# Moving feature transfers to two queues, and tile splits and gates to the first phase, in a gated mix of linear attention and a squared-relu MLP

## The chip, the cores and the metric

The kernel runs on one core of a Trainium2 chip. The metric is the device time of one execution in microseconds (us), lower is better; the time before is the median of three runs. All times below are in us unless another unit is given. TensorE (PE in the profile) multiplies matrices, VectorE (DVE) and GpSimd (POOL) do elementwise work, ScalarE (ACT) evaluates functions and copies, and SyncE (SP) only issues DMA transfers. DMA transfers can also be issued from ScalarE's and GpSimd's queues.

## What is computed

The sequence has 2048 rows of 512 numbers. With sigmoid, softmax over 16 numbers, and relu squared, the reference is, cut to what matters:

```python
g = sigmoid((x * gate_w).sum(-1, keepdims=True))
q, k, v = heads(x @ wqkv)                       # 32 heads of 16
pq, pk = q @ w_phi, k @ w_phi                   # per head, 16 x 16
phi_q = concat(softmax(pq), softmax(-pq))       # 32 features per head
phi_k = concat(softmax(pk), softmax(-pk))
kv = einsum("sf,sd->fd", phi_k, v); z = phi_k.sum(rows)
a = ((phi_q @ kv) / (phi_q @ z + 1e-6)) @ wo
h = relu(x @ w1 + b1) ** 2                      # 2048 x 1792
out = g * a + (1 - g) * (h @ w2 + b2)
```

## The kernel before

A product of two fp32 matrices is made of three matmuls (`mm3`): each operand is split into a high part (rounded to fp32r, ScalarE) and a low part (the rest, a subtraction on VectorE or GpSimd), and high x high, high x low and low x high are summed. `split` (line 391) does this for one 128 x 512 tile: one ScalarE copy and one subtraction.

The rows are four blocks of 512 (b = 0 to 3), the 1792 hidden columns 14 tiles of 128 (f = 0 to 13). The work has two phases.

The first phase makes two streams of products, both with a Strassen-like scheme of seven products over 2 x 2 blocks. The u stream (`u_step`, line 537) makes `h`: r = 0 gives blocks 0 and 1, then r = 1 blocks 2 and 3, and each step g of it gives two f (2g and 2g + 1) for two blocks, four tiles. `hidden` (line 531) finishes a tile: ScalarE takes relu with bias into a buffer named `row` (there are five), squares it in place, and SyncE stores it to DRAM (`hkept`). The v stream (`v_step`) makes the key features and values, and `kv_burst` sums their products in PSUM. Split w1 tiles are kept in DRAM (`wkept`) by r = 0 and loaded back by r = 1.

The second phase takes the blocks in the order 2, 3, 0, 1 (`ORDER_B`), and within a block the tiles in the order f = 2, 3, ..., 13, 0, 1 (`turned`). For each tile, `h_ready` (line 778) loads it from `hkept` into a buffer of a ring of four, and splits it into the operand buffers O0h, O0l, O1h, O1l (each twice, so that four tiles are held). `down` multiplies it with `w2`, four products of 128 rows each. Between these tiles lie the steps of the attention, by pairs p of 128-row chunks (two pairs in a block):

- `kv_done` (line 694): the summed keys and values go through DRAM (`zrow`) to be broadcast over the partitions (`vext`), and into the matrix `kvb`. Its four DMA transfers are on ScalarE's queue.
- `do_q` (line 801): the query product of a chunk and its exponentials `e` with their sums.
- `transposed` (line 811): `q_phi` multiplies `e` with `vext` on GpSimd (`ez`), VectorE sums it to the denominators (`dz`, `den`), scales `e` and transposes it in blocks of 32 into `tb`. After the second chunk of a pair, sixteen quarter-size pieces are carried from `tb` to `phiT`: four by a ScalarE copy (same partitions) and twelve by a DMA of 64 KB on SyncE's queue.
- `do_n` (line 829): 32 small matmuls of `kvb` with `phiT`, then a split; `attend` (line 853) multiplies the result with `wo` and adds it to the output row.
- `gates` (line 711), once for each block: four loads of `xn` (one buffer), for each a multiply with `gwb` and sum on VectorE, then sigmoid's exponential and a few small steps. `q_phi` of that block needs its results `inv` and `eps`.
- `wo_ready` (line 752): `wo` in four tiles, each made of four transfers of 64 KB (32 rows each), then split.

The program order is not the order of the engines. All operations are first added to a `Plan` (line 131), which walks a simulated clock with assumed lengths (`lengths`, line 191; `landing`, line 215, for transfers). Each operation gets a due time, counted back from the place of TensorE's products in program order; at each step of the clock, an engine takes the operation due soonest among those ready, and TensorE takes the earliest ready of the next five products (`LOOK`). An operation may have a choice of queues: `either` is VectorE or GpSimd. Loads from DRAM are held back until 45 before their due time (`HORIZON`), except those of `xn` (`op.early`); `gwb` is held back too. At most eight transfers are in flight in the plan. Each engine then runs its operations in the order so found, and waits in that order.

In the profile nearly all instructions have line 350, where the plan issues them, so tiles are told apart by name.

Of the kernel before, what the change touches and what calls it, by code (L numbers as in the profile page):

```python
# [17 lines left out]
P = 128  # L18
S, D, H, DH, F = 2048, 512, 32, 16, 1792
NK = D // P  # L20
SB = 512
# [11 lines left out]
LOOK = 5  # L33
HORIZON = 45.0


# [69 lines left out]
def region(ap):  # L106

    view = isinstance(ap, View)
    if not view and ap.space == DRAM:
        lo, hi = ap.offset, ap.offset + sum((c - 1) * s for s, c in ap.ap)  # L110
        return ap.tensor.name, lo, hi, 1
    width = ap.base.n if view else 1
    for n in () if view else ap.tensor.shape[1:]:
        width *= n
    p0, at = divmod(ap.offset, width)
    step, n = ap.ap[0]
    bits = 1
    for s, c in reversed(list(ap.ap)[1:]):
        if s:
            bits = sum(bits << k * s for k in range(c)) if s >= bits.bit_length() else any_of(bits, s, c)  # L120
    return ap.base.tag if view else ap.tensor.name, p0, p0 + (n - 1) * max(step // width, 1 if n > 1 else 0), bits << at

# [8 lines left out]
class Plan:  # L131
# [7 lines left out]
    def __init__(self, nc):  # L139
        self.nc, self.ops, self.seen, self.group = nc, [], {}, 0  # L140
        self.held, self.before = {}, {}
        self.tensor, self.vector, self.scalar = Queue(self, "tensor"), Queue(self, "vector"), Queue(self, "scalar")
        self.gpsimd, self.sync, self.either = Queue(self, "gpsimd"), Queue(self, "sync"), Queue(self, "vector", "gpsimd")
        self.const_aps = nc.const_aps

# [3 lines left out]
    def add(self, names, method, args, kw):  # L149
# [7 lines left out]
        op.size = max(free_size(a) for a in aps)  # L157
        op.early = method == "dma_start" and reads[0].space == DRAM and reads[0].tensor.name != "in_xn"
        wide = [a for a in reads if free_size(a) > 1]
# [31 lines left out]
    def lengths(self, op, engine):  # L191
        n = op.size
        if op.method == "dma_start":
            issue = {"sync": 0.45, "scalar": 0.36, "gpsimd": 0.7}[engine]
            return issue, issue
# [31 lines left out]
    def order(self):  # L227
# [74 lines left out]
        while len(done) < len(ops):  # L302
            best = None
            for e in ("vector", "scalar", "gpsimd", "sync"):
                for op in waiting[e]:
                    if op.start is not None:
                        continue
                    t = max(free[e], op.ready, op.due - HORIZON if op.early else 0.0)
                    if op.two:
                        t = max(t, lock)  # L310
                    if op.method == "dma_start" and len(flight) >= 8:
                        t = max(t, flight[-8])
                    if best is None or t < best[0] - 1e-9:
                        best = (t, e)
# [12 lines left out]
            for op in waiting[e]:  # L327
                s = max(free[e], op.ready, op.due - HORIZON if op.early else 0.0)
                if op.two:
# [33 lines left out]
def tile_gated_mix(ctx: ExitStack, tc: tile.TileContext, xT, xn, wqT, wkT, wphi, wv, wo, w1, b1, w2, b2, gw, out):  # L363
# [57 lines left out]
    wkept4 = dram.tile([NPF, 2, P, 256], F32, name="wkept4")  # L421
    hkept = dram.tile([NB, NF, P, SB], F32, name="hkept")
    vext = [const(f"vext{i}", H * VW + 32 - VW) for i in range(2)]
# [107 lines left out]
    def hidden(b, f, src, t=None):  # L531
        t = row() if t is None else t
        nc.scalar.activation(t, src, AF.Relu, bias=b1c[:, f:f + 1])
        nc.scalar.activation(t, t, AF.Square)
        nc.sync.dma_start(hkept[b, f], t)

# [215 lines left out]
    def wo_ready():  # L752
        tags = ("XS40h", "XS40l", "XS41h", "XS41l", "wo2", "O2l", "Vt5", "O2h")
        for k in range(NK):
            t = row()
            for q in range(4):
                s = 64 * (4 * (k % 2) + q) + 32 * (k // 2)
                nc.sync.dma_start(t[32 * q:32 * q + 32, :], wo[s:s + 32, :])
            hl = [operand(tag) for tag in tags[2 * k:2 * k + 2]]
# [51 lines left out]
    def transposed(p, c):  # L811
# [8 lines left out]
        for j in range(4):  # L820
            for r in range(4):
# [4 lines left out]
                else:  # L826
                    nc.sync.dma_start(dst, src)

# [268 lines left out]
```

## Time and profile before

| | |
|---|---|
| Median of three runs | 501.35 (500.74 to 501.95) |
| The profiled execution, its own time | 501.8 |
| Its span, first to last instruction | 500.0 |
| TensorE busy | 487.1 (97%) |
| VectorE busy | 396.6 (79%) |
| ScalarE busy | 254.6 (51%) |
| GpSimd busy | 153.1 (31%) |
| Moved by DMA | 91.87 MB, mean 184 GB/s |
| Mean granted TensorE clock | 0.993 |

A line of the timeline gives the start, the length, the engine, the operation and its tiles (written <- read). An engine's name with a q (SPq, ACTq) is its queue issuing a DMA. A row of the waits reads: who waited, for whom, total, times, longest. A row of a group gives the count, the total busy time and the mean in ns of one, then the idle time before it. A DMA group gives the size of one and the median time from issue to landing. The chain of waits is followed back from the last instruction, and shows in order of time what each step waited for.

### The profile page before, as it was taken

Reading aid. Unit: us, or ns where it says so; the run is one execution under the profiler, and the core shown is the slowest. Engines: PE = TensorE matmul, PEld = TensorE weight load, DVE = VectorE, ACT = ScalarE, POOL = GpSimd, SP = SyncE. Lnnn points to the kernel's source line nnn. Section 1 sums busy time; section 2 is a strip of 40 time slices with the busy share of each in tenths; the row PEclk is TensorE's granted clock in tenths of the full one; section 3 lists DMA queues with packets and bytes.
Section 4 is the critical chain, followed back from the end, with each engine's and each line's share of the span. In section 5 each row is a group of like instructions: output and inputs, shape, how many; then the busy total and the mean of one; then the engine's idle time right before and its main releaser. Section 6 shows DMA issues by size and latency. Waiting matters only on the chain.

```text
span 500.0 us, 9484 instructions
## 1 busy us (share of the span) xinstructions
PE 487.1 (97%) x3538; PEld 390.9 (78%) x3538; DVE 396.6 (79%) x572; ACT 254.6 (51%) x447; POOL 153.1 (31%) x129
## 2 busy tenths in 40 slices
PE   9999999999999999999999499998999999999997
PEld 4878888888888888888888277877878787878786
DVE  4997999778665746689989988899999988897323
ACT  5897966478554465689432344152444333344210
POOL 1022145048300000166277355243452524231000
PEclk9999999999999999999999899999999999999999
DMA  8999997434554783687644374436536330345302
GB/s 273 386 398 352 361 347 262 148 126 152 189 149 155 266 264 117 219 286 212 203 139 125 94 265 148 127 100 173 170 119 206 120 91 16 84 148 174 102 1 84
DMA packets 56518, 91.87 MB, mean 184 GB/s; under 512 B 7192, under 2 KB 16664, under 8 KB 56472
## 3 DMA queue, kind: packets, MB, share of 16 engines
q1 hardware_dynamic: 55536, 89.81, 54.8%
q10 hardware_dynamic: 904, 1.45, 0.9%
q8 instruction: 28, 0.46, 0.4%
q14 instruction: 18, 0.15, 0.1%
q0 software_dynamic: 32, 0.01, 0.0%
HBM read 51.91 MB, written 33.03 MB: 170 GB/s over the span
## 4 chain that ended last, share of the span: by engine, by line
PE 80%; DVE 7%; DMA 7%; ACT 2%; SPq 2%; issue 1%; POOL 0%; ACTq 0%; DVEq 0%; POOLq 0%
PE uB L350 21%; PE uA L350 12%; PE uE L350 12%; PE vB L350 11%; PE vA L350 9%; PE vE L350 9%; PE kv L350 6%; DMA row<-in_wo 2%; SPq L350 2%; DMA KT11l<-in_xT 1%; DVE e L350 1%; DMA wkept<-O0l 1%; DMA vext<-zrow 1%; DMA tb<-in_xT 1%; ACT row L350 1%
## 5 line engine op out<-in xcount | busy, mean ns | idle before, releaser
L350 POOL TENSOR_TENSOR ez<-e,vext 128x512 f32<-128x512 f32 x32 | 42.9, 1361 | 38.3 <-ACT e L350 28.7
L350 POOL TENSOR_TENSOR O1l<-ring,O1h 128x512 fp32r<-128x512 f32 x15 | 19.8, 1319 | 93.3 <-ACT O1h L350 92.5
L350 ACT ACTIVATE e<-e 128x512 f32<-128x512 f32 x54 | 31.4, 622 | 28.9 <-DVE e L350 28.9
L350 DVE TENSOR_REDUCE sm<-e 128x64 f32<-128x1024 f32 x27 | 32.8, 1215 | 10.5 <-ACT e L350 10.4
L350 ACT ACTIVATE O1h<-ring 128x512 fp32r<-128x512 f32 x33 | 20.7, 627 | 39.3 <-PE uB L350 13.4
L350 ACT ACTIVATE O0h<-ring 128x512 fp32r<-128x512 f32 x33 | 20.6, 626 | 31.2 <-PE uB L350 17.3
L350 ACT ACTIVATE row<-row 128x512 f32<-128x512 f32 x56 | 34.2, 626 | 0.6
L350 ACT ACTIVATE phiT<-tb 32x512 f32<-32x512 f32 x32 | 20.1, 629 | 23.9 <-DVE tb L350 23.6
L350 POOL TENSOR_TENSOR O0l<-ring,O0h 128x512 fp32r<-128x512 f32 x14 | 19.3, 1379 | 35.4 <-ACT O0h L350 35.4
L350 DVE TENSOR_TENSOR O1l<-ring,O1h 128x512 fp32r<-128x512 f32 x18 | 16.6, 919 | 11.6 <-ACT O1h L350 11.6
L350 DVE TENSOR_REDUCE ends<-vB 128x32 f32<-128x512 f32 x28 | 18.0, 680 | 8.7 <-PE vB L350 8.7
L350 DVE TENSOR_TENSOR O0l<-ring,O0h 128x512 fp32r<-128x512 f32 x19 | 15.4, 808 | 10.0 <-ACT O0h L350 10.0
L350 DVE TENSOR_REDUCE dz<-ez 128x64 f32<-128x1024 f32 x16 | 19.3, 1208 | 3.5 <-POOL ez L350 3.5
L350 DVE TENSOR_TENSOR e<-e,w 128x1024 f32<-128x1024 f32 x16 | 21.6, 1349 | 0.3
L350 DVE TENSOR_REDUCE ends<-vA 128x32 f32<-128x512 f32 x20 | 12.8, 681 | 10.2 <-PE vA L350 10.0
L350 DVE STREAM_TRANSPOSE tb<-e 128x1024 f32<-128x1024 f32 x16 | 19.7, 1232 | 0.0
L350 DVE RECIPROCAL r<-sm 128x64 f32<-128x64 f32 x32 | 17.4, 544 | 0.6
L350 DVE TENSOR_TENSOR e<-vB,ends 128x1024 f32<-128x1024 f32 x12 | 14.4, 1203 | 0.2
L350 DVE TENSOR_TENSOR e<-e,r 128x1024 f32<-128x1024 f32 x11 | 14.5, 1323 | 0.1
L350 DVE SCALAR_TENSOR_TENSOR xn<-xn,gwb 128x512 f32<-128x512 f32 x16 | 11.8, 736 | 1.2 <-DMA xn<-in_xn 1.2
L350 ACT ACTIVATE row<-uB,b1c 128x512 f32<-128x512 f32 x13 | 8.8, 680 | 6.9 <-PE uB L350 6.9
L350 ACT ACTIVATE row<-uA,b1c 128x512 f32<-128x512 f32 x13 | 8.9, 681 | 6.2 <-PE uA L350 6.1
(1132 smaller groups left out, 1650.7 us busy)
## 6 DMA issues: line engine op xcount, KB each, us to landing
hkept<-row SPq DMA_DIRECT2D x56, 256.0 KB, 3.9
ring<-hkept SPq DMA_DIRECT2D x56, 256.0 KB, 2.8
phiT<-tb SPq DMA_DIRECT2D x96, 64.0 KB, 2.0
xn<-in_xn SPq DMA_DIRECT2D x16, 256.0 KB, 3.2
out<-row SPq DMA_DIRECT2D x15, 256.0 KB, 3.5
ring<-in_w SPq DMA_DIRECT2D x11, 256.0 KB, 4.5
tb<-in_xT SPq DMA_DIRECT2D x8, 256.0 KB, 5.9
wkept<-O0h SPq DMA_DIRECT2D x6, 256.0 KB, 4.8
```

Of the source, the lines that this page charges most:

```text
L350: call(*map(real, op.args), **{k: real(a) for k, a in op.kw.items()})
```

## The change

- The twelve `phiT` transfers of a pair may be issued on SyncE's or ScalarE's queue (`nc.queues`); the plan chooses.
- `wo` comes in four transfers of 256 KB, each reading four blocks of 32 rows through a rearranged view, instead of sixteen of 64 KB.
- Loads of `xn` and `gwb` may start 160 before they are due. So far `xn` had no limit, and `gwb` 45, and the gates need both.
- 32 of the 56 tiles of `h` (blocks 2 and 3: f from 2 to 11; blocks 0 and 1: f from 8) are split in the first phase: after the square, a ScalarE copy into one of two slots (`b2b` and `wo2`, by turns of f // 2), a subtraction in place on VectorE or GpSimd, and two stores for one. The second phase loads both parts straight into the operand buffers.
- The plan's assumed length of a DMA issue on SyncE and ScalarE becomes 0.6 where the source's runs are shorter than 512 numbers, else 0.42 (so far 0.45 on SyncE and 0.36 on ScalarE).
- `region`, which tells the plan what an access touches, now counts further steps over partitions.

```diff
+PARTED = 8
...
     bits, more = 1, 0
     for s, c in reversed(list(ap.ap)[1:]):
-        if s:
+        if s >= width:
+            more += (c - 1) * (s // width)
+        elif s:
...
+        self.queues = Queue(self, "sync", "scalar")
...
-        op.early = method == "dma_start" and reads[0].space == DRAM and reads[0].tensor.name != "in_xn"
+        op.ahead = float("inf")
+        if method == "dma_start" and reads[0].space == DRAM:
+            op.ahead = 160.0 if reads[0].tensor.name in ("in_xn", "in_gw") else HORIZON
...
-            issue = {"sync": 0.45, "scalar": 0.36, "gpsimd": 0.7}[engine]
+            issue = 0.7 if engine == "gpsimd" else 0.6 if run_of(op.args[1]) < D else 0.42
...
-                    t = max(free[e], op.ready, op.due - HORIZON if op.early else 0.0)
+                    t = max(free[e], op.ready, op.due - op.ahead)
...
-    hkept = dram.tile([NB, NF, P, SB], F32, name="hkept")
+    hkept = dram.tile([NB, NF, 2, P, SB], F32, name="hkept")
...
         nc.scalar.activation(t, t, AF.Square)
-        nc.sync.dma_start(hkept[b, f], t)
+        if not parted(b, f):
+            nc.sync.dma_start(hkept[b, f, 0], t)
+            return
+        hi = slot(("b2b", "wo2")[f // 2 % 2], F32R)
+        split(t, hi, t.bitcast(F32R), nc.either)
+        nc.sync.dma_start(hkept[b, f, 0], ff(hi))
+        nc.sync.dma_start(hkept[b, f, 1], t)
+
+    def parted(b, f):
+
+        return 2 <= f < 12 if b >= 2 else f >= PARTED
...
             t = row()
-            for q in range(4):
-                s = 64 * (4 * (k % 2) + q) + 32 * (k // 2)
-                nc.sync.dma_start(t[32 * q:32 * q + 32, :], wo[s:s + 32, :])
+            blocks = wo.rearrange("(t q r i) n -> t r q i n", t=2, q=4, r=2)
+            load(t, blocks[k % 2, k // 2])
...
-        split(load(ring(), hkept[b, f]), hi, lo, nc.either)
+        if not parted(b, f):
+            split(load(ring(), hkept[b, f, 0]), hi, lo, nc.either)
+            return
+        for j, o in enumerate((hi, lo)):
+            nc.sync.dma_start(ff(o), hkept[b, f, j])
...
-                    nc.sync.dma_start(dst, src)
+                    nc.queues.dma_start(dst, src)
```

More of the change, by code (lines that the diff above doesn't have):

```diff
@@ L116, in region @@
     step, n = ap.ap[0]
-    bits = 1
+    bits, more = 1, 0
     for s, c in reversed(list(ap.ap)[1:]):
-        if s:
+        if s >= width:
+            more += (c - 1) * (s // width)
+        elif s:
             bits = sum(bits << k * s for k in range(c)) if s >= bits.bit_length() else any_of(bits, s, c)
-    return ap.base.tag if view else ap.tensor.name, p0, p0 + (n - 1) * max(step // width, 1 if n > 1 else 0), bits << at
+    return ap.base.tag if view else ap.tensor.name, p0, p0 + more + (n - 1) * max(step // width, 1 if n > 1 else 0), bits << at
 def any_of(bits, s, c):
@@ L327, in order @@
             for op in waiting[e]:
-                s = max(free[e], op.ready, op.due - HORIZON if op.early else 0.0)
+                s = max(free[e], op.ready, op.due - op.ahead)
                 if op.two:
```

## The prediction

> **What bounds the kernel now.** I read the page first, then busy time by stretch, TensorE's waits, the chain of waits, and the timeline where the chain leaves TensorE.
>
> ```profile
> span 500.0 us, 9484 instructions
> PE 487.1 (97%) x3538; PEld 390.9 (78%) x3538; DVE 396.6 (79%) x572; ACT 254.6 (51%) x447; POOL 153.1 (31%) x129
> ```
>
> TensorE idles for only 12.9 us of the span, so nothing that relieves another engine counts unless it removes some of these. The next view says where they lie: per stretch its length, then busy time of PE, PEld, DVE, ACT and POOL, the granted clock, the DMA share and GB/s.
>
> ```profile
> 0.00:37.50 37.50, 36.03 (x139) 25.67 (x140) 28.95 (x51) 29.84 (x54) 5.77 (x17) 1.00 0.97 352
> 37.50:65.00 27.50, 27.50 (x242) 22.53 (x241) 23.33 (x39) 24.50 (x46) 7.50 (x6) 1.00 0.98 361
> 65.00:140.00 75.00, 75.00 (x819) 61.72 (x818) 61.97 (x77) 45.52 (x82) 31.59 (x27) 1.00 0.56 191
> 140.00:225.00 85.00, 85.00 (x741) 70.04 (x740) 55.45 (x77) 51.33 (x89) 9.66 (x7) 1.00 0.65 214
> 225.00:278.65 53.65, 53.65 (x479) 43.83 (x477) 49.31 (x68) 26.61 (x48) 28.84 (x22) 1.00 0.51 159
> 278.65:290.20 11.55, 4.71 (x39) 2.57 (x39) 10.48 (x14) 4.63 (x9) 5.11 (x4) 0.70 0.57 165
> 336.50:340.00 3.50, 2.14 (x35) 0.86 (x35) 3.50 (x6) 0.63 (x1) 2.46 (x2) 1.00 0.69 167
> 487.50:500.00 12.50, 9.29 (x47) 7.73 (x45) 4.68 (x7) 0.00 (x0) 0.00 (x0) 1.00 0.22 84
> ```
>
> The idle time is 1.47 at the start, 6.84 in one hole after 278.65, 1.36 near 338 and 3.21 at the end. Start and end are not touched by the change. The two holes in between are what can be won, and the waits of TensorE name their cause:
>
> ```profile
> PE vB L350 <- DMA phiT<-tb: 3.8, 1, 3.8
> PE vE L350 <- DMA phiT<-tb: 3.1, 1, 3.1
> PE vE L350 <- DVE den L350: 1.4, 1, 1.4
> ```
>
> Both are `do_n`, which multiplies the rearranged query features `phiT` with `kvb`. The timeline of TensorE prices the large hole in full:
>
> ```profile
> 278.42 0.39 PE L350 MATMUL kv<-XS31h,XA221l 128*128 128x512 f32 x1
> ...
> 290.20 0.39 PE L350 MATMUL uE<-KB221h,O1l 128*128 128x512 f32 x1
> 290.43 0.40 PE L350 MATMUL uB<-KB221h,O1h 128*128 128x512 f32 x1
> ```
>
> Matmuls of 512 columns start 0.23 apart, so TensorE was free at 278.65 and was back in step at 290.20, 11.55 later. In between lie a `do_n` and five matmuls. A `do_n` with its data there takes about 1.0 (next fence, first start of its main part to the next product), five matmuls 1.15. So 9.4 is lost: 6.84 as idle time, the rest because the granted clock was 0.70 over the stretch and work ran slowly after the waits.
>
> ```profile
> 338.85 0.37 PE L350 MATMUL vE<-phiT,kvb 64*32 64x256 f32 x1 [1.36 <-DVE den L350]
> ...
> 339.87 0.50 PE L350 MATMUL uA<-KB211h,O1h 128*128 128x512 f32 x1
> ```
>
> What `do_n` waited for is in the chain of waits, and in the timeline of SyncE:
>
> ```profile
> 242.57 5.74 DMA vext<-zrow
> ...
> 251.51 2.30 POOL ez L350 x2
> ...
> 284.11 2.04 DMA phiT<-tb
> ```
>
> ```profile
> 276.93 7.77 SPq L350 DMA_DIRECT2D phiT<-tb  x12
> ```
>
> The summed keys and values (`vext`) land at 248.31; GpSimd starts the denominators at 251.51; SyncE has the transposed features at 276.93 and issues twelve transfers one after another, 0.65 each; the last is issued at 284.11 and lands at 286.15. That is 7.5 after TensorE was free.
>
> **The change part by part.** The twelve `phiT` transfers may go on SyncE's or ScalarE's queue. ScalarE also makes four copies of the same rearrangement, 0.63 each (the row of the first below), 2.5 in all.
>
> ```profile
> 276.94 0.63 ACT L350 ACTIVATE phiT<-tb 32x512 f32<-32x512 f32 x1 [5.80 <-DVE tb L350]
> ```
>
> If ScalarE makes its copies and issues four transfers (2.5 + 4 x 0.65 = 5.1) while SyncE issues eight (5.2), the queue ends 2.6 sooner. The bounds are 0 (the planner leaves all on SyncE) and 3.9 (six and six, the copies hidden); I take 2.6. What ScalarE does behind an issue is evictions and exponentials; it was busy 26.61 of 53.65 before the hole, so there is room.
>
> The Trainium skill speaks against this part: DMA: Bandwidth & Descriptors, section Issuing engines are not separate DMA queues, says that all issuers share the same 16 DMA engines and that a second issuer saves only issue time, which is usually small beside the transfer. Here the rows say otherwise, 7.77 of issue against 2.04 of flight. By the rule the 2.6 would be close to 0.
>
> Twenty of the 32 tiles that are split early are those of blocks 2 and 3 with f from 2 to 11, and the second phase starts with block 2 at f = 2. So its first ten tiles need no split. The gates leave this place as well. Two rows from the stretch between `vext` and the transposition, in which VectorE has hardly a gap:
>
> ```profile
> 256.68 1.44 DVE L350 TENSOR_TENSOR O1l<-ring,O1h 128x512 fp32r<-128x512 f32 x1
> ...
> 259.29 0.68 DVE L350 SCALAR_TENSOR_TENSOR xn<-xn,gwb 128x512 f32<-128x512 f32 x1
> ```
>
> These two are 2.1 on the chain and both go. The bounds are 0 (the list fills the place with something due sooner) and 4 (a second split and GpSimd's splits go too; the 1.44 is dearer than the mean below, so the two engines slow each other here). I take 2.1 and 0.5 for the last point.
>
> `wo` comes in four transfers of 256 KB for sixteen of 64 KB. Between `vext` landing and the first denominator lie 3.2, in which GpSimd stood behind the split of a `wo` tile. I take 1.8 of it, since another GpSimd job of 1.4 (the mean of one further below) may stand there; bounds 3.2 and -2 (if the `wo` tiles come later, ScalarE's copy of them holds what is queued behind it: `zrow`, `vext` and the exponentials).
>
> Sum for the hole: 2.6 + 2.1 + 0.5 + 1.8 = 7.0 of 7.5. So `do_n` is 0.5 late and waits too little to lose the clock (the 1.36 near 338 left it at 1.00). Gain 9.4 - 0.5 = 8.9.
>
> The 1.36 near 338 is named for VectorE, but there too twelve transfers stood on SyncE:
>
> ```profile
> 329.38 7.62 SPq L350 DMA_DIRECT2D phiT<-tb  x12
> ```
>
> They end at 337.00, and with 2.04 of flight at 339.0, which is when `do_n` went on (338.85). With 2.6 less this wait goes: 1.4.
>
> The new work in the first phase: 32 copies on ScalarE, 32 subtractions on VectorE or GpSimd, 32 more stores, 8.4 MB.
>
> ```profile
> L350 ACT ACTIVATE O0h<-ring 128x512 fp32r<-128x512 f32 x33 | 20.6, 626 | 31.2 <-PE uB L350 17.3
> ...
> L350 POOL TENSOR_TENSOR O0l<-ring,O0h 128x512 fp32r<-128x512 f32 x14 | 19.3, 1379 | 35.4 <-ACT O0h L350 35.4
> L350 DVE TENSOR_TENSOR O1l<-ring,O1h 128x512 fp32r<-128x512 f32 x18 | 16.6, 919 | 11.6 <-ACT O1h L350 11.6
> ```
>
> That is 32 x 0.63 = 20 on ScalarE and 29 (all on VectorE) to 44 (all on GpSimd). The twenty tiles of blocks 2 and 3 fall mostly into 140 to 225, where ScalarE was busy 51 of 85 and GpSimd 10 of 85; the twelve of blocks 0 and 1 (from f = 8) mostly into 65 to 140, where ScalarE was busy 46 of 75 and GpSimd 32 of 75. The 16 gate steps (16 x 0.68 = 11) find room on VectorE there too; their 16 loads go out on SyncE between the stores, and the one of `gwb` on ScalarE, a few tenths each, with a queue that is mostly empty in front of them. The cover is thin only before 65, where the DMA engines were at 0.98. I charge 0.7, half of what TensorE idled in the busiest part (1.47 before 37.5); bounds 0 and 3. In the second phase 32 tiles take two loads for one load and a split: one more issue of some 0.4 on SyncE, behind which stand `phiT` and the stores of the output, while SyncE loses half of its `phiT` issues.
>
> All together: 501.8 (the profiled execution: span 500.0 and 1.8 around it) - 8.9 - 1.4 + 0.7 = 492.2. The median of the three runs is 0.45 below the profiled one, which gives **491.8**. The floor, with both holes gone and half the idle of the start, is 501.8 - 9.4 - 1.4 - 0.7 - 0.45 = 489.8.
>
> **The rivals.** First, `do_n` stays late. Without a gain from the second queue (chance 0.06) 2.6 and the 1.4 come back, 495.8, and some 1.5 (of the 9.4 - 6.84 = 2.6) more if the wait grows past 3 and the clock drops as it did after the waits of 3.8 and 3.1: 497.3. The rows of issue and flight speak against it. Or `wo` is late (chance 0.13):
>
> ```profile
> hkept<-row SPq DMA_DIRECT2D x56, 256.0 KB, 3.9
> ```
>
> An ordinary 256 KB transfer is issued once and lands in 3.9. But the new source of `wo` is a view of four blocks of 32 rows. If it moves on four of the 16 DMA engines, each carrying 65.5 KB at 23 GB/s (361 GB/s at a share of 0.98, by 16), one transfer takes 2.85 and four in line 11.4, twice the 5.74 of `vext`, with ScalarE's copies, and what is queued behind them, waiting for it. The term of 1.8 goes, or turns into -2, and behind a wait of over 3 the clock drops as well: 493.6 to 497.5.
>
> The Trainium skill, DMA: Bandwidth & Descriptors, section Why a DMA increments its semaphore by 16 and not by 1, states such a rule: the engines used are the largest number up to 16 that divides the outermost size of both sides, which is 4 here. No transfer of before shows it at this size.
>
> Second, the other side: the early splits stall the first phase. The high halves use two slots, and the four tiles of one step of f share one. Two of them are stored 1.2 apart:
>
> ```profile
> 148.29 0.38 SPq L350 DMA_DIRECT2D hkept<-row  x1
> 148.76 0.38 SPq L350 DMA_DIRECT2D O1l<-wkept  x1
> 149.49 0.32 SPq L350 DMA_DIRECT2D hkept<-row  x1
> ```
>
> The slot is held for 0.63 of copy, 0.38 of issue and 3.9 to landing, 4.9 together, so the second tile's copy must stand 3.7 back. If ScalarE waits there in order, evictions wait behind it: two such waits, 7.4, in each of 8 groups. It decides once TensorE feels 1.3 of a group's 7.4 (10.3 of gain by 8); if it feels a quarter, 1.85, it is 15 in all and the time 491.8 + 15 = 506.8. For it: ScalarE's order is fixed beforehand and 3.9 is a median. Against it: the planner knows of the store and puts the copy behind it, ScalarE has 34 free of 85 there, and TensorE did not wait once after 37.5 in this phase.
>
> Third, nothing much: the new order of the list opens other holes at later `do_n` or at the change of phase, as large as those it closes, 498 to 501.5.
>
> **How the numbers follow.** Forecast (490 to 493.5) 0.65; `do_n` late (493.5 to 498) 0.19; nothing much 0.08; slower 0.08. The range to 497 takes in the forecast and most of the first rival. About 0.2%, 1 us, is what a measurement can tell, since the three runs lie 1.2 apart. Half of the third case is faster by that: faster 0.87, same 0.04, slower 0.09.
>
> **What would show it.** Right: no wait of TensorE on `phiT` above 1 us, the twelve transfers of a pair over in about 5 on two queues, PE clock 1.00 after 280, first ten loads of the second phase without a copy behind them, TensorE's idle time 3 to 5. Wrong: a wait of over 2 at the first `do_n`; ScalarE standing for `wo` for several us around 240; waits of TensorE between 60 and 225 after ScalarE's copies, above all in groups of f.

## The result and the profile after

The changed kernel takes 508.11 (median of four runs, 507.64 to 509.88) where the kernel before took 501.65 beside it (four runs, 500.74 to 502.37). The ratio is 1.0124, 95% interval 1.0090 to 1.0158: about 6.2 us slower, where 491.8 was forecast. The profiled execution took 508.11.

The page of the changed kernel, first lines:

```profile
span 506.3 us, 9599 instructions
PE 490.6 (97%) x3538; PEld 391.6 (77%) x3538; DVE 384.2 (76%) x567; ACT 250.5 (49%) x447; POOL 159.7 (32%) x134
```

TensorE idles for 15.7 (12.9 before), and its busy time grew by 3.5 although it runs the same 3538 matmuls. Part of that is the granted clock: it was 0.50 for 10.2 in all (3.4 each from 233.1, 287.7 and 455.0), where before it was 0.50 for 6.8 (from 283.1); this makes 1.7 of the 3.5, and where the rest comes from is not shown. Busy time by stretch shows the places (the columns are those of the prediction):

```profile
140.00:225.00 85.00, 84.21 (x733) 68.36 (x734) 60.75 (x93) 57.62 (x102) 22.14 (x17) 1.00 0.83 277
225.00:240.00 15.00, 12.53 (x246) 9.67 (x248) 11.59 (x19) 9.97 (x20) 8.66 (x8) 0.89 0.76 257
262.00:278.00 16.00, 14.28 (x62) 11.26 (x61) 14.75 (x24) 1.78 (x3) 7.36 (x6) 1.00 0.56 170
278.00:291.00 13.00, 10.71 (x66) 7.58 (x65) 7.45 (x10) 7.09 (x13) 3.88 (x4) 0.87 0.77 238
448.00:460.00 12.00, 10.06 (x64) 7.13 (x63) 10.96 (x16) 5.05 (x9) 5.49 (x4) 0.86 0.68 202
```

The one large hole at the first `do_n` has become smaller, and four places that were full before have holes: the end of the first phase (225 to 240), 268, 308 and 451. To put a number on each, I took TensorE's timeline and summed, from the start of each row to the start of the next, what goes beyond 0.227 for a 512-column product, 0.12 for 256 columns and 0.04 for smaller ones. This lost time holds the waits and the slow clock; where small products stand close together a row is good to some tenths:

| Stretch | Before | After |
|---|---|---|
| 0 to 62 | 5.5 | 5.2 |
| 62 to 225 | 1.4 | 3.0 |
| 225 to 262 | 0.8 | 4.4 |
| 262 to 275 | 0.0 | 2.2 |
| 275 to 295 (first `do_n`) | 9.9 | 5.2 |
| 295 to 330 | 0.9 | 2.6 |
| 330 to 345 | 2.7 | 0.9 |
| 345 to 440 | 2.7 | 2.6 |
| 440 to 462 | 0.9 | 4.8 |
| 462 to the end | 0.9 | 0.9 |
| sum | 25.7 | 31.8 |

The difference, 6.1, accounts for the 6.3 by which the span grew. The smaller loss at the first `do_n` is no gain, though. Its features are complete at 286.89, later than before (286.15), and TensorE only comes to it later, after the losses ahead of it:

```profile
283.74 0.39 PE L356 MATMUL uB<-KB220h,O0l 128*128 128x512 f32 x1
...
287.03 0.37 PE L356 MATMUL vE<-phiT,kvb 64*32 64x256 f32 x1 [1.25 <-DMA O0h<-hkept]
```

TensorE was free for it at 283.97, 5.3 later than before (278.65). Up to 295 the changed kernel has lost 20.0, the kernel before 17.6. The waits of TensorE name different causes, none of them of the size of before:

```profile
PE vB L356 <- DVE e L356: 2.5, 1, 2.5
PE uA L356 <- ACT O1h L356: 1.9, 1, 1.9
PE uA L356 <- DMA O1h<-hkept: 1.7, 1, 1.7
PE uA L356 <- ACT ring L356: 1.4, 1, 1.4
PE vE L356 <- DMA O0h<-hkept: 1.3, 1, 1.3
PE vB L356 <- ACT phiT L356: 1.0, 1, 1.0
```

The row that names the load O0h is that of 287.03, and the name is wrong: `do_n` reads only `phiT` and `kvb`. The last of this pair's `phiT` transfers was issued by ScalarE at 283.18, and the trace's record of semaphores has it landed at 286.89. So two of these waits, 1.3 and 1.0, are for `phiT`.

Four of the places were followed to their beginnings. First the middle, 240 to 290, in the chain of waits of the changed kernel:

```profile
241.00 10.11 DMA row<-in_wo
...
251.12 9.03 DMA row<-in_wo
...
261.36 1.35 DVE KT41l L356
...
263.85 0.62 DVE xn L356 x2
...
264.91 5.08 DMA O1h<-hkept
```

Two transfers of `wo`, 10.11 and 9.03 for 256 KB each, lead straight to the wait at 268: the copy of the last `wo` tile, behind it on ScalarE the copy KT41h, its subtraction on VectorE, an `e` and a gate step there, the next `xn` load on SyncE that waits for the gate step's buffer, and behind that the load O1h for which TensorE waits. ScalarE's own timeline shows what stood behind `wo` there:

```profile
247.91 0.63 ACT L356 ACTIVATE XS41h<-row 128x512 fp32r<-128x512 f32 x1 [4.13 <-DMA row<-in_wo]
247.92 0.53 ACTq L356 DMA_DIRECT2D zrow<-kvs  x1
251.13 0.63 ACT L356 ACTIVATE XS40h<-row 128x512 fp32r<-128x512 f32 x1 [2.58 <-DMA row<-in_wo]
252.99 0.83 ACTq L356 DMA_DIRECT2D vext<-zrow  x2
255.09 0.63 ACT L356 ACTIVATE wo<-row 128x512 fp32r<-128x512 f32 x1 [3.33 <-DMA row<-in_wo]
...
260.17 0.63 ACT L356 ACTIVATE Vt<-row 128x512 fp32r<-128x512 f32 x1 [3.40 <-DMA row<-in_wo]
...
278.54 5.25 ACTq L356 DMA_DIRECT2D phiT<-tb  x7
283.84 2.56 ACT L356 ACTIVATE phiT<-tb 32x512 f32<-32x512 f32 x4 [15.09 <-DMA phiT<-tb]
```

ScalarE stood 13.4 for `wo` in four waits. The second `zrow` transfer went out only when the wait for the first tile was over, so `vext`, which reads `zrow` and was issued at 242.57 before, is issued at 252.99. The last two rows are the first pair's `phiT`: ScalarE issued seven transfers in 5.25 and made its own four copies behind them, which were over at 286.40. SyncE had its five out by 281.86. Starts and landings of the twelve:

```profile
L356 ACTq DMA_DIRECT2D phiT<-tb x7: 607/639/845, 278.5 to 283.2; - x7
L356 SPq DMA_DIRECT2D phiT<-tb x5: 589/611/751, 278.5 to 281.3; - x5
DMA to landing us min/median/max: 2.1/2.1/3.7
```

The longest landing, 3.7, is that of the last issue at 283.18: the last piece was there at 286.89.

Second, the end of the first phase. ScalarE, then VectorE, of the changed kernel:

```profile
228.14 0.63 ACT L356 ACTIVATE KB211h<-KT30l 128x512 fp32r<-128x512 f32 x1 [3.38 <-DMA KT30l<-in_w]
228.68 0.19 ACT L356 ACTIVATE ge<-lg 128x4 f32<-128x4 f32 x1
```

```profile
228.90 1.28 DVE L356 TENSOR_SCALAR inv<-ge 128x4 f32<-128x4 f32 x1 [2.16 <-ACT ge L356]
...
230.38 1.26 DVE L356 TENSOR_REDUCE ends<-vB 128x32 f32<-128x512 f32 x2
```

A weight load (KT30l) held ScalarE's copy for 3.38. The gates' exponential `ge` stood behind that copy, the gates' small steps on VectorE waited for `ge`, and behind them stood `ends` and `e`, which free the PSUM bank for which TensorE waits. Third, the hole at 308, ScalarE and then TensorE:

```profile
307.43 2.17 ACTq L356 DMA_DIRECT2D phiT<-tb  x3
309.64 0.69 ACT L356 ACTIVATE ring<-uA,rest 128x512 f32<-128x512 f32 x1 [3.92 <-PE vE L356]
```

```profile
310.38 0.50 PE L356 MATMUL uA<-KB110h,O0h 128*128 128x512 f32 x1 [1.42 <-ACT ring L356]
```

Three `phiT` issues, 0.72 each, stood ahead of an eviction; before them ScalarE had waited for the tile `tb` that they read, which VectorE finished at 307.41. Fourth, the hole at 451, in the chain of waits:

```profile
437.65 0.61 ACTq L356
...
440.88 1.16 ACT e L356 x2
...
442.16 2.56 POOL ez L356 x2
...
449.58 2.90 DMA ring<-hkept
...
452.50 0.64 ACT O1h L356
```

It starts with six `phiT` issues on ScalarE from 434.05 to 438.27. Behind them stand its own four `phiT` copies, the exponentials `e`, GpSimd's `ez`, VectorE's denominators and a `row` step that frees a ring buffer, the load into that buffer, and the copy O1h for which TensorE waited 1.9.

### The profile page after: what moved, and what is told of

It is laid out like the page before. It is cut to its first block, busy times and chain, and to the rows that moved or that the text cites. A ratio compares the mean times of both kernels' runs of the same rounds, so it can differ in the third digit from the quotient of the medians.

```text
span 506.3 us, 9599 instructions
## 1 busy us (share of the span) xinstructions
PE 490.6 (97%) x3538; PEld 391.6 (77%) x3538; DVE 384.2 (76%) x567; ACT 250.5 (49%) x447; POOL 159.7 (32%) x134
## 4 chain that ended last, share of the span: by engine, by line
PE 69%; DMA 15%; DVE 6%; ACT 4%; issue 3%; ACTq 1%; SPq 1%; POOL 1%; DVEq 0%; POOLq 0%
PE uB L356 19%; PE uA L356 11%; PE uE L356 11%; PE vB L356 9%; PE vA L356 7%; PE vE L356 6%; PE kv L356 6%; DMA row<-in_wo 4%; ACT row L356 1%; DMA wkept<-O0h 1%; DMA O0h<-hkept 1%; DMA KT30l<-in_w 1%; DMA KT30h<-in_w 1%; ACTq L356 1%; DMA ring<-in_w 1%
## 5 line engine op out<-in xcount | busy, mean ns | idle before, releaser
L356 POOL TENSOR_TENSOR ez<-e,vext 128x512 f32<-128x512 f32 x32 | 44.3, 1405 | 89.2 <-ACT e L356 77.3
L356 ACT ACTIVATE O0h<-ring 128x512 fp32r<-128x512 f32 x17 | 10.5, 625 | 30.6 <-DMA phiT<-tb 10.2
L356 POOL TENSOR_TENSOR row<-row,wo 128x512 fp32r<-128x512 f32 x10 | 13.4, 1340 | 37.7 <-ACT wo L356 36.6
L356 POOL TENSOR_TENSOR row<-row,b2b 128x512 fp32r<-128x512 f32 (+1 forms) x9 | 11.9, 1317 | 24.0 <-issue 15.3
L356 POOL TENSOR_TENSOR O0l<-ring,O0h 128x512 fp32r<-128x512 f32 x9 | 11.7, 1298 | 22.9 <-ACT O0h L356 22.9
L356 ACT ACTIVATE wo<-row 128x512 fp32r<-128x512 f32 x17 | 10.7, 629 | 14.8 <-DMA hkept<-wo 9.0
L356 POOL TENSOR_TENSOR O1l<-ring,O1h 128x512 fp32r<-128x512 f32 x7 | 9.3, 1323 | 19.9 <-ACT O1h L356 17.4
L356 DVE TENSOR_TENSOR O1l<-ring,O1h 128x512 fp32r<-128x512 f32 x10 | 7.8, 781 | 9.1 <-ACT O1h L356 9.1
L356 DVE TENSOR_TENSOR row<-row,b2b 128x512 fp32r<-128x512 f32 (+1 forms) x13 | 10.1, 778 | 5.9 <-ACT b2b L356 5.9
L356 ACT ACTIVATE O1h<-ring 128x512 fp32r<-128x512 f32 x17 | 10.7, 628 | 7.4 <-PE uB L356 4.0
```

The source lines that it names most:

```text
L356: call(*map(real, op.args), **{k: real(a) for k, a in op.kw.items()})
```

## The experiments

Two theories were set against each other. The first: the four-block view of `wo` moves slowly, and ScalarE, which copies `wo` in order, stands for it. The second: ScalarE's share of the `phiT` issues delays its copies, exponentials and evictions. Beside them stood the early splits and the early gates, each of which fills the first phase. All ratios are to the kernel before on the same chip, with 95% intervals; a difference of two ratios is turned into us at 501, and its half-width is worked out from the two intervals (root of the sum of squares).

### The source of wo

Flat `wo`: the host lays the rows of `wo` out so that each tile is 128 whole rows, and the kernel loads them plainly. What is computed stays the same, but the layout is made ahead of the launch.

```diff
-            blocks = wo.rearrange("(t q r i) n -> t r q i n", t=2, q=4, r=2)
-            load(t, blocks[k % 2, k // 2])
+            s = P * (2 * (k % 2) + k // 2)
+            load(t, wo[s:s + P, :])
...
-        "wo": A_wo,
+        "wo": A_wo.reshape(2, 4, 2, 32, D).transpose(0, 2, 1, 3, 4).reshape(D, D),
```

**The changed kernel with flat wo.** Every engine runs the same instructions in the same order as in the changed kernel; only the source of four transfers differs.

> The changed kernel with one difference: the host lays wo out so that each of its four transfers reads 128 rows in a line, instead of four blocks of 32 rows; all engines have the same order as in the changed kernel. Theory A (the four-block view moves on few DMA engines, one transfer takes 9 to 10 us instead of some 4, ScalarE stands for it in order, and the summed keys and values come 10 us late): the four waits of ScalarE for wo (4.1, 2.6, 3.3, 3.4) fall under 1.5 each, vext lands some 6 to 10 sooner, the holes near 268 and 284 to 291 (1.9 and 5.5) shrink, and the time falls from 508.1 to 500 to 503. Theory B (the loss comes from the DMA volume of the early splits and from ScalarE issuing transfers, wo only shows it): the waits may shrink but the time stays above 506.

Measured 501.17, ratio 0.9994 (0.9963 to 1.0025): 6.5 ± 2.3 less than the changed kernel. The DMA group of `wo`:

```profile
row<-in_wo SPq DMA_DIRECT2D x4, 256.0 KB, 5.5
```

5.5 to landing (3.2 to 7.5 singly), where the four through the view took 8.3 to 10.1 in the changed kernel. The holes at 268 and at the first `do_n` are gone (lost time 0.0 and 0.9); those at the end of the first phase (1.6), 302 (2.9) and 447 (2.4) are left.

**The kernel before with the four-block view, and with flat wo.** Nothing else of the change is in them, and the two have the same order on all engines. The view replaces the three lines with the inner loop by the two lines shown above with a minus.

> The kernel before with one part of the change alone: wo in four transfers, each reading four blocks of 32 rows. Theory A: a transfer takes 9 to 10, the keys and values come late, the hole at the first do_n grows by some 5: 505 to 509. If the four-block view is slow only beside the stores of the early splits: 501, no change.

> The kernel before with wo in four transfers that read 128 rows in a line (laid out by the host), nothing else. My term of 1.8 for four transfers instead of sixteen: the first denominator starts nearer to the landing of vext, the hole at the first do_n (9.4 lost) shrinks by 2 to 4: 497 to 500. If sixteen small transfers were no hindrance: 501.

The view gave 500.16, ratio 0.9975 (0.9952 to 0.9997), flat 493.34, ratio 0.9868 (0.9800 to 0.9936): 5.4 ± 3.6 between them. The four flat runs lie far apart, 491.71 to 499.27, and the profiled one is the fastest of them; so this is the least certain size here. The 505 to 509 that I expected of the view did not come. One row of the chain with the view, then the DMA group with flat `wo`:

```profile
241.78 9.45 DMA row<-in_wo
```

```profile
row<-in_wo SPq DMA_DIRECT2D x4, 256.0 KB, 4.2
```

So four transfers through the view are 1.3 ± 1.1 better than sixteen small ones in the kernel before; the same four from whole rows are 6.6 ± 3.4 better. The landing time, not the number of transfers, is what counts. The issue of `vext` moves with it, at 247.51 with the view and at 244.01 with flat `wo`.

**wo later.** If the damage were only that `vext` stands behind `wo`, then loading `wo` later, so that its copies come after `vext`, would cure it. The loads of `in_wo` are held until 25 before they are due (else 45), in the kernel before with the view, in the changed kernel, and in the kernel before with flat `wo`.

```diff
+        op.ahead = 25.0 if op.early and reads[0].tensor.name == "in_wo" else HORIZON
...
-                    t = max(free[e], op.ready, op.due - HORIZON if op.early else 0.0)
+                    t = max(free[e], op.ready, op.due - op.ahead if op.early else 0.0)
```

> The kernel before with the four-block wo transfers, which may start only 25 before they are due instead of 45, so that ScalarE's copies of wo come after its issue of vext. This separates two ways in which a slow wo can hurt. If it hurts because ScalarE waits for it in order, ahead of vext: the slow transfers stay 9 long, but vext lands near 244 to 246, the first denominators start 5 or more sooner and the time is that of the flat wo, 492 to 495. If it hurts because the transfers queued behind it on the same DMA engines come late: 499 to 502 as with the four-block wo at the old place.

> The same limit of 25 in the changed kernel, its four-block wo and two queues kept. ScalarE's order as the cause: about the time of the flat wo there, 500 to 503. The DMA engines as the cause: 506 to 509.

> The kernel before with wo laid out flat (each transfer 128 whole rows) and its loads held to 25 before their due time; ScalarE's order is the same as in the kernel before with the four-block view held to 25 (503.43), so only the source of the four transfers differs. If the slow view alone makes ScalarE stand (first theory), the waits for wo at ScalarE shrink from 1.9 to 4.0 each to under 2, the phiT transfers start at 270 to 273 instead of 279.8, and the time is 493 to 497. If the late place of wo's copies is what costs, whatever the transfers take (second theory), phiT still starts near 279 and the time is 500 to 504.

The view, late, in the kernel before: 503.43, ratio 1.0038 (1.0019 to 1.0057). Flat, late: 497.90, ratio 0.9944 (0.9924 to 0.9964). In these two every engine's order is the same by name. `vext` went out at 242.85 and 242.15, so its delay is cured in both, yet ScalarE stood for the view at the later place. Copy of the last tile and the issue of the first twelve `phiT`, with the view:

```profile
268.30 0.63 ACT L351 ACTIVATE Vt<-row 128x512 fp32r<-128x512 f32 x1 [1.86 <-DMA row<-in_wo]
```

```profile
L351 SPq DMA_DIRECT2D phiT<-tb x12: 587/595/751, 279.8 to 287.1; - x12
```

and with flat `wo`:

```profile
261.34 0.63 ACT L351 ACTIVATE Vt<-row 128x512 fp32r<-128x512 f32 x1
```

```profile
L351 SPq DMA_DIRECT2D phiT<-tb x12: 585/595/744, 273.9 to 281.1; - x12
```

The exponentials behind the copies are late by 6.8 (269.88 and 263.09), and `phiT` by 5.9. The view costs 4.7 ± 1.4 here too. The late place costs by itself as well: flat and late is 3.8 ± 3.6 worse than flat and early. So the flat late run, 497.9, lies between the two ranges expected of it. In the changed kernel the late place gave 511.92, ratio 1.0203 (1.0174 to 1.0233), worse again by 4.0 ± 2.3. So the idea that the time comes back when `vext` is freed fell: `vext` was only one of the things behind `wo`.

### Two queues for phiT

```diff
-                    nc.queues.dma_start(dst, src)
+                    nc.sync.dma_start(dst, src)
```

**The changed kernel with all phiT on SyncE.**

> The changed kernel with all twelve phiT transfers of a pair on SyncE's queue again. Theory A: wo still holds the start, so little is won there, 506 to 510 in all. Theory C (ScalarE's issues of 0.6 to 0.9 each stand before its copies, evictions and exponentials, and make the holes near 308 and 450, 6.2 together): these holes go and the time is 501 to 503. If issuing on two queues pays as I forecast, the time rises to 510 or more.

Measured 502.78, ratio 1.0030 (1.0009 to 1.0052): 4.7 ± 2.0 less. The holes at 308 and 451 are gone, which fits the rows above (the order of the list changes with it, too); those at 230 (1.6), 268 (2.0) and 284 (2.4) are left.

**Both: flat wo and one queue.**

> The changed kernel with wo laid out flat and all phiT transfers on SyncE: the two causes found so far undone together. If they are two causes (wo 7, ScalarE's issues 5, with 2 of the 5 in the hole that wo made): 497 to 499, TensorE's holes near 302 and 448 of the flat kernel (2.9 and 2.4) gone. If ScalarE's issues only cost where ScalarE had already been held by wo: 500 to 502, as with the flat wo alone.

Measured 495.86, ratio 0.9879 (0.9853 to 0.9905), 12.3 ± 2.1 less than the changed kernel. The two costs add up within their intervals (6.5 and 4.7), so they are two causes and not one. The largest loss left in the middle was that at the end of the first phase: TensorE's longest wait is 2.3 for VectorE's `e`.

**The kernel before with two queues alone**, first with the plan's old lengths of an issue (0.36 on ScalarE), then with the new ones (0.6 where the source's runs are short).

> The kernel before with one part alone, phiT transfers on two queues. My forecast: the hole at the first do_n shrinks by 2.6 and the clock is kept, 496 to 499. Theory C (ScalarE puts its copies and exponentials behind the issues, so little is won at the first do_n and other holes open): 500 to 504.

> The kernel before with the phiT transfers on two queues and the plan's new lengths of an issue (0.6 and 0.42), wo as before and no early splits or gates. If the 523.6 of two queues alone came from the old length of 0.36 that made the plan put 70 of 96 on ScalarE (first theory), ScalarE now gets 40 to 60, its waits for phiT fall from 68 to under 50, and the time is 500 to 508. If phiT on ScalarE's queue costs by itself, at any share (second theory), the time stays over 508. If the second queue gains as forecast, 497 to 500.

Measured 523.60, ratio 1.0421 (1.0394 to 1.0447), and 510.76, ratio 1.0191 (1.0166 to 1.0216). With the old length the plan gives ScalarE 70 of the 96 transfers, with the new one 55. The first lies above every range that was expected, the second in the range for the case that issues on ScalarE cost by themselves. The first pair on ScalarE with the old lengths, then, with the copies, with the new ones:

```profile
277.90 5.55 ACTq L351 DMA_DIRECT2D phiT<-tb  x8
```

```profile
276.02 4.63 ACTq L351 DMA_DIRECT2D phiT<-tb  x7
280.70 2.56 ACT L351 ACTIVATE phiT<-tb 32x512 f32<-32x512 f32 x4 [9.68 <-DMA phiT<-tb]
```

0.69 and 0.66 each, and both times the copies come after them. With the new lengths the pair was complete at 283.30, 2.9 sooner than before (286.15; 1.9 of it in the 7.3 that the pair took for 9.2), which is about the forecast's 2.6. It did not help: the lost time at the first `do_n` is no smaller than before, since TensorE had come to it sooner, and new losses stand at 423 and 453, with waits of 2.4, 1.4 and 1.3. The wrong length explains about half: with the new lengths, which are close to these rows, two queues still cost 9.6 ± 1.2. In every run with the second queue the copies of the first pair stood behind the issues.

### Early splits

```diff
-        return 2 <= f < 12 if b >= 2 else f >= PARTED
+        return False
```

**Without them** in the changed kernel, and in the one with flat `wo` and one queue; then **they alone** in the kernel before.

> The changed kernel with no tile split in the first phase. Theory B: the holes near 182, 209 and 228 to 236 (1.1 and 4.2) go since 8.4 MB less are stored there, time 502 to 504 or lower. Theory A: the wo transfers are still slow and the second phase has its splits again, time 506 to 510.

> As the run before, without the early splits as well: what is left of the change is the gates in the first phase, four wo transfers and the plan's issue costs. If the early splits cost TensorE in the first phase (the waits at 183, 190 and 211 of the flat kernel, 2.8 together) and give nothing back later: 1 to 3 less than the run before. If they relieve VectorE in the second phase as I forecast: 2 to 5 more, with a wait at the first do_n back.

> The kernel before with one part alone, the 32 early splits. My forecast: some 2.6 less for the first do_n, 0.7 more in the first phase, 498 to 500. If the stores hold ScalarE and VectorE at the end of the first phase (as the holes of the changed kernel at 182, 209 and 228 to 236, 5.3): 502 to 506.

Without them the changed kernel takes 504.82, ratio 1.0070 (1.0044 to 1.0096), 2.7 ± 2.1 less: the hole at 230 goes, those at 308 and 451 too, and the lost time at the first `do_n` is 11.0. Beside flat `wo` and one queue it is the other way, 498.78, ratio 0.9918 (0.9876 to 0.9959), 2.0 ± 2.5 more, which is not apart from nothing. Alone they give 503.47, ratio 1.0045 (1.0019 to 1.0070): the first `do_n` gains, but a new hole of 7.0 opens at 370, where ScalarE has a gate step ahead of evictions (the profiled execution, 507.28, is the slowest of ten, so the hole is probably larger in it than in the others):

```profile
375.19 0.20 ACT L350 ACTIVATE ge<-lg 128x4 f32<-128x4 f32 x1 [10.77 <-DVE xn L350]
```

**With flat wo**: the new lengths without the splits, and the splits with the old lengths.

> The kernel before with flat wo and the plan's new lengths of an issue, phiT on SyncE, no early splits, no early gates: against the flat kernel with the splits (492.96) only the early splits are missing, against flat wo alone (493.34) only the lengths differ. If the early splits are worth what they were beside the early gates (2.9), the time is 495 to 497. If the splits gain only where the gates have filled VectorE and SyncE (rival), it is 491 to 494, and neither the splits nor the lengths matter once wo lands in time.

> The kernel before with flat wo and the early splits, old lengths: the early splits alone gave 503.47, with a new hole of 7 near 370 where ScalarE stood for a gate step. If that hole belongs to the splits' order of the list (first theory), it comes again and the time is 494 to 500, above flat wo alone. If it came from the late do_n with the slow wo (second theory), it is gone and the time is 489 to 493, the fastest of all.

Measured 496.07, ratio 0.9884 (0.9849 to 0.9920), and 493.12, ratio 0.9836 (0.9790 to 0.9882). Neither can be told from flat `wo` alone (0.9868). The hole of 7.0 at 370 does not come again (0.5 there), so it did not come from the splits as such; that it came with the order of the list that goes with the sixteen small transfers is argued, not shown. The new lengths alone change nothing that can be seen.

### Early gates

```diff
-            op.ahead = 160.0 if reads[0].tensor.name in ("in_xn", "in_gw") else HORIZON
+            op.ahead = float("inf") if reads[0].tensor.name == "in_xn" else HORIZON
```

**Undone** in the changed kernel; **alone** in the kernel before; **undone** beside flat `wo` and one queue.

> The changed kernel with the loads of xn and gwb held as before (xn free, gwb 45 before it is due), so that the gates fall into the second phase again. Theories A, B and C all expect no gain: 507 to 511. If the gates' loads and steps in the first phase are what delays its end (the hole at 228 to 236, 4.2), the time falls to 504.

> The kernel before with the loads of xn and gwb allowed 160 before they are due, and nothing else: gates in the first phase. If the gate row that leaves VectorE's chain is worth its length (first theory, the term of 0.7 in the forecast's 2.1), the hole at the first do_n shrinks by 0.5 to 1.5 and the time is 500.3 to 501.5. If the gate steps that wait for their loads in order stall evictions (second theory, as in the run with the early splits alone), new holes of 2 to 7 open and the time is 503 to 508.

> The changed kernel with flat wo, all phiT on SyncE and the gates again unlimited for xn and 45 for gwb: against the same with early gates (495.86) only the gates differ. First theory: early gates are worth 1 to 3 here too, 497 to 499. Second theory: the loss that is left at the end of the first phase (2.6 at 229) comes from the gates' 16 loads and VectorE steps; then it goes without them, and the time is 493 to 495.

Undone in the changed kernel: 505.65, ratio 1.0090 (1.0061 to 1.0118), 1.7 ± 2.2 less, which is not apart from nothing. Alone: 505.63, ratio 1.0085 (1.0057 to 1.0112), 4.3 ± 1.4 slower. The hole at the first `do_n` shrinks from 9.9 to 7.5, but one of 4.3 opens at 370, where a copy for which the load came late stands ahead of `phiT` and of the evictions `ring`:

```profile
371.59 0.63 ACT L352 ACTIVATE XS10h<-ring 128x512 fp32r<-128x512 f32 x1 [5.14 <-DMA ring<-in_xT]
```

Undone beside flat `wo` and one queue: 492.96, ratio 0.9846 (0.9826 to 0.9866), 1.7 ± 1.6 less than with them. ScalarE still stood for KT30l there,

```profile
225.33 0.63 ACT L356 ACTIVATE KB211h<-KT30l 128x512 fp32r<-128x512 f32 x1 [2.44 <-DMA KT30l<-in_w]
```

but with no gate step in line behind it the wait of TensorE for `e` is gone; its two longest waits are now 1.4 for an eviction into `ring` and 1.1 for VectorE.

Several versions beat both kernels. The three lowest cannot be told from each other: the kernel before with flat `wo` (493.34), the same with early splits (493.12), and the changed kernel with flat `wo`, one queue and late gates (492.96). All three take `wo` in whole rows, laid out ahead of the launch, and keep `phiT` on SyncE.

## Why the prediction was wrong, point by point

**What bounds the kernel.** Right: TensorE's few idle places decide, and the kernel before gains 6.6 when the one at the first `do_n` is closed (flat `wo`: lost time there 2.1 for 9.9). The floor of the forecast, 489.8, is what the lowest versions come near.

**"If ScalarE makes its copies and issues four transfers ... the queue ends 2.6 sooner."** This step failed. The plan gave ScalarE 54 of the 96 transfers, and for the first pair seven issues ahead of its four copies, so the pair took 8.4 (278.49 to 286.89) where it had taken 9.2 (276.93 to 286.15): 0.8 sooner, and not 2.6. At 308 and 451 the loss is gone once ScalarE issues none; it is gone as well when ScalarE issues and the early splits are left out, so it takes both. I wrote that "there is room" on ScalarE because it was busy half of the time. Room counts only if it lies at the right moment, in an order that is fixed. The term of 2.6 was in truth a cost of 4.7 ± 2.0.

The 1.4 at 338 came, but not from the second queue: that wait is gone as well with all `phiT` on SyncE, and with nothing but the view of `wo`. I had also added it up wrongly, the flight to the end of the last issue. From its start, as for the large hole, the transfers are there at 338.4, and the profile names VectorE's `den`, which ended at 338.51.

The Trainium skill, DMA: Bandwidth & Descriptors, section Issuing engines are not separate DMA queues, which I set aside, says that a second issuer saves only issue time. The trace agrees, 0.8 being part of the issue time, and goes further: the issue time is moved onto an engine that also computes.

**"I take 1.8 of it" for wo in four transfers.** Alone in the kernel before, the number came out, 1.3 ± 1.1, but by luck. The first denominator began later there, not sooner (253.53 for 251.26), and the first `do_n` still waited 3.4 and 3.0; what went is the wait at 338. In the changed kernel `wo` is issued from 239.56 on (233.67 before), takes 8.3 to 10.1 to land, and holds ScalarE for 13.4; the first denominator begins 10.9 later than before.

My first rival had this mechanism, at a chance of 0.13 and at 493.6 to 497.5. Its size failed: I put 2.85 for one transfer and 11.4 for all, and from the first issue to the last landing it was 20.6. (The upper bound of that rival adds up to 497.1 from its own terms of 1.8, 2 and 1.5.) The rule of the Trainium skill that I named there (same page, section Why a DMA increments its semaphore by 16 and not by 1) is borne out. In all runs with the view 256 KB took 6.5 to 12.3, from 128 whole rows 3.2 to 7.5. And the kept traces hold each update of the semaphore that tells of a landing: 16 for every transfer of whole rows, but five for every one through the view. The one issued at 239.56 has an update at 240.69 and four from 247.26 to 247.89; if each engine in use counts once at its end, that is four engines. The 23 GB/s for each engine I took from a stretch with a DMA share of 0.98. Four engines that carry the four tiles in 20.6 move 12.7 GB/s each, an estimate from these rows; other transfers ran beside them.

**"These two are 2.1 on the chain and both go."** The rows did leave VectorE, and the lost time at the first `do_n` fell from 9.9 to 7.5 with the early gates alone, to 6.8 with the splits alone. In size the term was too small. From the first denominator to the first `phiT` issue (276.93 before, 278.49 after) it was 25.7 and is 16.4 now:

```profile
251.26 2.54 POOL L350 TENSOR_TENSOR ez<-e,vext 128x512 f32<-128x512 f32 x2
```

```profile
262.12 3.48 POOL L356 TENSOR_TENSOR ez<-e,vext 128x512 f32<-128x512 f32 x2
```

That is 9.3 less, where I had 2.1 and 0.5 (with the splits alone it is 5.8 less, with the gates alone 2.2; with flat `wo` alone 3.2, so not all of it need be splits and gates). The delay by `wo` ate all of it. Two gate steps stand in that stretch still, at 263.8 and 271.3, and a tile that needs no split can be waited for as a load (268, 1.7): the load came late in SyncE's line.

**"I charge 0.7" for the first phase.** This failed worst in size: lost time from 62 to 262 went from 2.2 to 7.4, that is 5.2 for 0.7. I had looked for work that lies beside other work, by busy shares. The largest piece, at 230, came from order: a weight load landed late, after 6.0, and a gate step moved to an earlier place made VectorE wait in line for ScalarE. That the load was late because stores and loads filled the DMA engines (0.83 from 140 to 225, 0.65 before) is argued, not shown. I counted the gates' 11 on VectorE and named their loads, but not who waits behind them.

**The slower rival.** Its mechanism was the slot of the split tile. ScalarE did wait for those stores, 9.0 in five waits for one slot and 7.9 in four for the other, but TensorE waited only 0.8 for the tile (vB) that stood behind such copies. The slowdown is real, by other ways.

**The clock.** "`do_n` is 0.5 late and waits too little to lose the clock" failed in its first half: `do_n` waited 1.0 and 1.3 between 283.97 and 287.03, and then the clock was 0.50 for 3.4:

```profile
287.70:291.10 3.40, 3.40 (x21) 2.20 (x8) 2.91 (x4) 3.40 (x7) 3.40 (x4) 0.50 1.00 349
```

The same followed the waits of 2.5 (to 233.4) and 1.9 (to 453.2). It did not follow the single waits of 1.7 at 268 and 1.4 at 308 (1.00 in the rows from 262 to 278 above and from 291 to 330), as it had not followed the 1.36 near 338. So the prediction was right about a wait like that one, but its price for a wait of over 3 was due from far shorter waits on.

Added up by the lost time, against the forecast: the first `do_n` gained 4.7 for 8.9 (4.2 missing), 338 gained 1.8 for 1.4, the first phase cost 4.5 more than charged, and 268, 308 and 451 cost 2.2, 1.7 and 3.9 that I had at nothing. That is 16.1; the two stretches left out give back 0.4, and the forecast's 0.45 from the profiled execution to the median comes on top, which makes about the 16.3 between 491.8 and 508.1. The rows say where time is lost, not what caused it: the 4.7 at the first `do_n` is loss that had moved to the places ahead of it.

**What stays open.** How much of the slow `wo` is the four engines themselves, and how much the traffic beside them; whether two queues could gain in a list that puts ScalarE's copies ahead of its issues, which was not tried; and the worth of the early splits, which is within what the runs can tell once `wo` lands in time.

## What to carry to other kernels

An engine that runs in a fixed order pays for each thing it issues or waits for with everything behind it, so before moving a DMA, a copy or an early step there, read from the timeline what stands behind it at that moment; a busy share of 50% says nothing about that. Price a transfer by a transfer of the same shape, or test the shape alone: here one line, the layout of a small weight, was worth 6.6 ± 3.4 us in the kernel before, and no part of the change alone brought more than 1.3. Where several edits are put together, run each alone as well: three of the four here cost time by themselves.

## What was not expected of the hardware

- 256 KB through a view of four blocks of 32 rows landed in 8.3 to 10.1 in the changed kernel and 7.1 to 9.5 in the kernel before, from 128 whole rows in 3.2 to 7.5 and 4.1 to 5.4, at about the same places; the semaphore of a landing was updated 5 times for the view and 16 times for whole rows. One issue took 0.53 to 0.74 with the view, and mostly 0.33 to 0.43 with whole rows (0.85 at most).
- An issue of a 64 KB transfer between 32-partition pieces took, with the gap to the next, 0.66 to 0.75 on ScalarE's queue (seven in 4.63 and in 5.25), and 0.65 to 0.67 on SyncE's (twelve in 7.77, five in 3.37).
- In all kept traces, each TensorE wait of 1.8 or more between 10 and 480 went with a granted clock of 0.50 for 3.4, or two or three times that (the shortest, 1.84, twice in the run with one queue). No single wait of 1.1 to 1.4 did, two of 1.7 went one each way (changed kernel at 268 not, with late `wo` at 234 yes), and pairs of 1.0 to 1.4 close together did in three places. That is too few for a threshold.
